# Single score banks for VectorE between ScalarE's rounds, in an attention and gated GLU kernel

## The chip, the cores and the metric

The kernel runs on one core of one Trainium2 chip. The metric is the device time of one execution in microseconds (us), lower is better. TensorE (PE), VectorE (DVE), ScalarE (ACT), GpSimd (POOL) and SyncE (SP) each work through a program of their own in order; PSUM, where TensorE's results land, is counted here in banks of 128 x 512 fp32 numbers, and there are eight.

## The reference

```python
xn = _layernorm(A_x)                       # x: 1 x 2048 x 640
# attention: 32 heads of 20
qkv = (xn @ wqkv).reshape(B, S, 3, H, Dh).transpose(2, 0, 3, 1, 4)
scores = einsum("bhqd,bhkd->bhqk", q, k) * Dh ** -0.5
o = einsum("bhqk,bhkd->bhqd", softmax(scores), v)
s = o.transpose(0, 2, 1, 3).reshape(B, S, D) @ wo
# gated GLU, F = 1728
h = sigmoid(xn @ w_gate) * (xn @ w_up)
g = silu(h @ w_down)
out = A_x + s * g
```

## The kernel before, in words

After a setup of about 30 us (layer norm, transposed activations in `xnT`, the first keys, queries and values) the main part runs over 32 passes: 4 chunks of 512 queries by 8 groups of 4 heads. A pass has 16 tiles of 128 keys for each of its 4 heads, so 64 **score banks** of 128 keys x 512 queries; 2048 in all (`NB`; the last pass is cut in two parts of 256 queries). Each bank is made by TensorE (`score`, L1155; the 4 heads lie in four groups of rows of the array, which can work side by side), turned into probabilities, and used by TensorE again (`pv`, L1289, "PV"), which adds probabilities times values in the bank `oacc`.

The exponential is made by one of two engines:

- **ScalarE**, in **rounds** (`issue`, `act_exp`): TensorE fills 3 or 2 banks in turns (`sc0`, `sc1`), and one instruction makes the exponential of all of them (L1177).
- **VectorE** (`dve_exp`): four instructions on one bank, each reading what the one before wrote. L1188 (`bits`, writes `dy`) reads the score bank and sets it free, L1193 and L1197 (`square`, `cube`, write `du`) and L1201 (`power`, writes `p`) work in SBUF.

Five PSUM banks belong to the rounds and one is `oacc`. The other two, `misc0` and `misc1`, are **shared**: a score bank for VectorE (named `spare`) takes one until L1188 has read it, and everything else that TensorE does takes one too (named `work`): keys, queries and values of later groups, the GLU's gate and up products (L644, L657), its down product (L680) and the output projection (L719, L751). A gate product's bank is freed by ScalarE's tanh (L651), most others by an eviction on VectorE (an up product by L661, which writes `hT`). The taker is `take_bank`, the freeing `give_bank`.

The order of all instructions is written by a planner in the kernel's Python, which keeps a clock for TensorE (`pe[0]`) and models VectorE and ScalarE (`Engine`: a queue of tasks, each with a length, what it depends on and a rank; the task that can start first goes first, at equal start the lower rank). A VectorE step of 512 columns counts 606 ns, with 114 ns more until a result can be used; a matmul of 512 columns counts 216 ns (`MM5`), a change between scores, PV and other work 100 ns (`INTO`); an exponential its columns / 1.2 + 52 ns. `dve.backlog` is the sum of the queued tasks' lengths, `dve.t` the time at which the running one ends.

At each step the main loop does the first of these that is possible: a round, when ScalarE's next PSUM set is free and ScalarE is about to run dry (`until` is the time at which the round is due, `room` what is left until then); a PV batch; one matmul of other work (`fill`), paced by a credit that every score bank issued adds to; a matmul on zeros that keeps TensorE's clock up (`zero_add`, L1265); else the clock moves on.

VectorE's score banks are issued in rounds alone: `issue` adds one behind ScalarE's 2 or 3, when VectorE has less than `D_BACKLOG` (2500 ns) of work and a shared bank is free. Which bank it is says `dve_bank`: the lowest of the heads' next banks that the round hasn't taken, none close to a pass's end (`NEEDED`), where one of the next pass is taken if its keys and queries are there. So that a round finds a bank, `spare_wanted` keeps other work from the last free one when the next round is near (within 800 ns, later 400) and VectorE's queue short.

Of the kernel before, what the change touches and what calls it, by code (L numbers as in the profile page):

```python
# [45 lines left out]
def kernel(  # L46
# [322 lines left out]
    MM5, MM3, MM1 = 216.0, 136.0, 70.0  # L369
# [41 lines left out]
    pe = [0.0]  # L411
# [19 lines left out]
    def pe_do(kind, took, streamed=None):  # L431
        if mode[0] != kind:
            pe[0] += INTO[kind]
            mode[0] = kind
        pe[0] += took
        if took:
            streams.append((pe[0], took if streamed is None else streamed))
# [14 lines left out]
    def take_bank(name="work"):  # L452
        ready = [i for i in range(2) if banks[i].t is not None and banks[i].t <= pe[0]]
        if not ready:
            return None
        i = min(ready, key=lambda i: banks[i].t)
        banks[i] = Cell()
        return i, psum.tile([P, QC], FP32, tag=f"misc{i}", bufs=1, name=name)
# [7 lines left out]
    def give_bank(held, cell):  # L466
        banks[held] = cell
# [603 lines left out]
    def per_bank(b):  # L1071
        todo, most = 0.0, 0.0
        for x in sorted(flight + jobs, key=lambda x: x.due):
            todo += max(0.0, x.left)
            most = max(most, todo / max(1.0, x.due - b))
        return most
# [2 lines left out]

    KEEP_SPARE, KEEP_LATE, SPARE_END, next_round = 800.0, 400.0, 20 * PER_PASS, [0.0]  # L1080
    BUFS, D_BACKLOG = {3: 4, 2: 4, 1: 3}, 2500.0
    NEEDED, NEEDED_LAST = 6, 12
    PV_TIME = 2 * MM5 + 30.0
    sets = [Cell(0.0), Cell(0.0)]
    buffers = {n: [Cell(0.0)] * BUFS[n] for n in BUFS}
# [23 lines left out]
    def lacks():  # L1109
        return list({(w[1], w[2]): w for b in coming(GH) for w in needs(b)}.values())  # L1110

    def issued(b):
        j = b % GH
        done_ahead[j].add(b // GH)
        while ahead_of[j] in done_ahead[j]:
            done_ahead[j].remove(ahead_of[j])
            ahead_of[j] += 1

    def dve_bank(banks):
        b = min((x for x in coming(GH) if x not in banks), default=None)  # L1120
        if b is None:
            return None
        ends = PER_PASS * (b // PER_PASS + 1) if b < LAST else min(e for e in ENDS if e > b)
        if ends - b > (NEEDED if ends < NB else NEEDED_LAST):
            return b
        if ends == NB:
            return None
        b = ends + b % GH
        while b // GH in done_ahead[b % GH]:
            b += GH  # L1130
        cells = [w[0].get(w[1]) for w in needs(b)]
        if any(c is None or c.t is None or c.t > pe[0] for c in cells):
            return None
        return b
# [15 lines left out]
    def score(ps, b):  # L1150
        p, r = divmod(b, PER_PASS)
        qc, g = steps[p]
        j, rows = r % GH, slice(32 * (r % GH), 32 * (r % GH) + 1 + Dh)
        for kt, q0, c0, n in pieces(b):
            nc.tensor.matmul(ps[:, c0:c0 + n], lhsT=kT_all[rows, g, kt * P:(kt + 1) * P],  # L1155
                             rhs=qTs[qc, g][rows, q0:q0 + n], start=True, stop=True, tile_position=(32 * j, 0))
# [25 lines left out]
    def dve_exp(ps, b, begun):  # L1182
        buf = Probs([b], "p1")
        t = {}

        def bits():
            t["y"] = pp.tile([P, 512], FP32, tag="dy", bufs=2, name="dy")
            nc.vector.tensor_scalar(out=t["y"], in0=ps, scalar1=LEAST, scalar2=None, op0=ALU.max)  # L1188
            t["f"] = t["y"].bitcast(U16).rearrange("p (q two) -> p q two", two=2)[:, :, 0]

        def square():
            t["u"] = pp.tile([P, 512], FP32, tag="du", bufs=2, name="du")
            nc.vector.scalar_tensor_tensor(out=t["u"], in0=t["f"], scalar=CUBE_2, in1=t["f"],  # L1193
                                           op0=ALU.add, op1=ALU.mult)

        def cube():
            nc.vector.scalar_tensor_tensor(out=t["u"], in0=t["u"], scalar=CUBE_1, in1=t["f"],  # L1197
                                           op0=ALU.add, op1=ALU.mult)

        def power():  # L1200
            nc.vector.scalar_tensor_tensor(out=buf.tile()[:, 0, :].bitcast(U16), in0=t["u"], scalar=CUBE_SCALE,  # L1201
                                           in1=t["y"], op0=ALU.mult, op1=ALU.add)

        first = dve.add(606.0, [Cell(begun + MM5 + PE_OUT - 100.0), *d_made[-2:-1]], bits, 0, 114.0)
        c = dve.add(606.0, [first, *d_made[-2:-1]], square, 3, 114.0)
        c = dve.add(606.0, [c], cube, 3, 114.0)
        buf.made = dve.add(606.0, [c, buf.before], power, 3, 114.0)
        d_made.append(buf.made)
        return first

    def issue():
# [23 lines left out]
        at_bank[0] += n  # L1235
        return n

    def pv_batch():

        p = pv_pass[0]  # L1240
        if p >= len(steps) - 1 + len(PARTS):
            return None
        if sum(pv_count[0]) == 0 and not (oacc_free[0].t is not None and oacc_free[0].t <= pe[0]):
            return None
        batch = []
        for j in range(GH):
            mine = []
            for x in ready_p[j]:
                b, buf, i = x
                if unit(b) > p or len(mine) == 2:  # L1250
                    break
                c, v = buf.made, v_cells.get((b % PER_PASS // GH, steps[min(p, len(steps) - 1)][1]))
                if c.t is not None and c.t + SEM <= pe[0] and v is not None and v.t is not None and v.t <= pe[0]:
                    mine.append(x)
            if len(mine) < 2:
                return None
            batch.append(mine)
        return batch
# [61 lines left out]
    while pv_pass[0] < len(steps) - 1 + len(PARTS):  # L1320
        advance(pe[0])
        pads()
        load_wo()
        load_bulk()
        ci, b0 = chunk[0], at_bank[0]
        p = min(b0, NB - 1) // PER_PASS
        until, stuck, can = 1e18, False, False
        if b0 < NB:
            wanted = lacks()
            late = [w[2] for w in wanted if w[0].get(w[1]) is None]  # L1330
            if late:
                must_fill(max(min(late) - 1, 0))
                continue
            cells = [w[0][w[1]] for w in wanted] + [sets[ci % 2]]
            stuck = any(c.t is None for task in act.queue for c in task[3])
            guess = pe[0] + (2000.0 if stuck else 400.0)
            free = max(c.t if c.t is not None else guess for c in cells)
            dry = max(act.t, pe[0]) + sum(t[2] for t in act.queue) - MM5 - PE_OUT + 2000.0 * stuck
            into = 0.0 if mode[0] == "score" else INTO["score"]
            until = max(free, dry - AHEAD) - into  # L1340
            can = all(c.t is not None for c in cells) and free <= pe[0] + into + 1.0
            if can and (until <= pe[0] + (0.0 if mode[0] == "score" else 40.0) or idle):
                idle = False
                n = issue()
                credit = min(credit + n * per_bank(b0), 3000.0)
                continue
        room = until - pe[0]
        next_round[0] = until
        held = sum(len(q) for q in ready_p)
        batch = pv_batch()  # L1350
        cost = PV_TIME + (INTO["pv"] if mode[0] != "pv" else 0.0)
        if batch and (cost <= room or held >= HELD):
            pv(batch)
            idle = False
            continue
        least = (0.0 if mode[0] == "fill" else INTO["fill"]) + MM3
        hurry = (b0 >= NB or stuck or any(x.due < b0 + URGENT for x in flight + jobs[:1])
                 or held >= 12 and lacks_v())
        if (credit > 0.0 or hurry) and least <= room:
            took = fill(p, room)  # L1360
            if took:
                credit -= took
                idle = False
                continue
        if b0 < NB and can and not idle:
            idle = True
            continue
        soon = [q[k][1].made.t for q in ready_p for k in range(min(2, len(q)))]
        due = min([t for t in soon if t is not None], default=pe[0]) if b0 >= NB else 1e18
        if zero_add(min(room, due - pe[0] - MM5)):  # L1370
            idle = False
            continue
        times = [until, pe[0] + 150.0] + [t + SEM for t in soon if t is not None]
        pe[0] = min(t for t in times if t > pe[0] + 1.0)
# [79 lines left out]
```

## Time and profile before

| | |
|---|---|
| time, median of 3 runs | 894.33 us (893.8 to 894.76) |
| time of the profiled execution | 894.27 us |
| its span | 892.1 us |
| busy: PE, DVE, ACT, POOL | 804.6, 840.7, 870.6, 162.0 us |
| ScalarE's exponentials (L1177) | 717, 827.9 us busy |
| VectorE's score banks (L1188) | 257 |
| granted TensorE clock | 0.998 |

The span is the time from the first to the last instruction of the profiled execution; the 2.2 us between it and that execution's time lie around it. A group's line gives the source line, engine and operation, what it writes and reads, shapes and count, then the busy time (overlaps counted once), the mean length of one instruction in ns, the idle time of the engine just before, and what ended it. An instruction's length reaches to its end, and the next of the same engine may start a little earlier, so lengths add up to more than the busy time. A line of waits gives who waited, for whom, the total in us, how often, and the longest.

### The profile page before, as it was taken

The page shows a single profiled execution, that of the slowest core. Times are in us where ns is not written, and L with a number is a line of the kernel's source. Part 1 is how long each engine was busy: PE and PEld are TensorE (multiplying, and loading weights), DVE is VectorE, ACT ScalarE, POOL GpSimd, SP SyncE. Part 2 cuts the span into 40 slices and gives each one's busy share as a digit, 9 for nine tenths or more (in the row PEclk, how much of TensorE's full clock was granted, in tenths as well). Part 3 has the DMA queues.
Part 4 walks back from the last instruction along what each step waited for, and adds up shares of the span by engine and source line. Part 5 has one row for each costly group of instructions (what it writes and reads, how often), then busy time and mean ns, then how long its engine had stood idle before and what let it go on. Part 6 is the DMA issues. An engine that isn't in the chain of part 4 may idle for free.

```text
span 892.1 us, 16911 instructions
## 1 busy us (share of the span) xinstructions
PE 804.6 (90%) x6227; PEld 290.3 (33%) x6310; DVE 840.7 (94%) x1487; ACT 870.6 (98%) x837; POOL 162.0 (18%) x305
## 2 busy tenths in 40 slices
PE   5899899998999999999899998989999898999896
PEld 3344333332223333232233332223333332233333
DVE  7799999999999999997999999999999989999997
ACT  6999999999999999999999999999999999999995
POOL 7401111111111212111101221101112220111121
PEclk9999999999999999999999999999999999999999
DMA  8113231135451234223212243313113432200012
GB/s 317 46 35 90 64 109 35 52 98 150 109 133 42 64 89 69 65 59 72 64 23 79 70 81 79 71 26 77 34 45 85 108 54 70 67 17 21 14 32 71
DMA packets 107672, 64.40 MB, mean 72 GB/s; under 512 B 80350, under 2 KB 101906, under 8 KB 107498
## 3 DMA queue, kind: packets, MB, share of 16 engines
q1 hardware_dynamic: 97382, 47.21, 19.8%
q0 software_dynamic: 10208, 16.11, 8.2%
q8 instruction: 49, 0.80, 0.4%
q14 instruction: 33, 0.27, 0.1%
HBM read 50.45 MB, written 16.13 MB: 75 GB/s over the span
## 4 chain that ended last, share of the span: by engine, by line
ACT 64%; issue 18%; PE 10%; DVE 7%; DMA 0%; SPq 0%; DVEq 0%; ACTq 0%
ACT p L1177 59%; PE sc L1155 3%; ACT tnh L651 3%; PE oacc L1289 2%; DVE dy L1188 2%; PE work L644 1%; DVE du L1193 1%; PE work L124 1%; PE work L680 1%; ACT td L691 1%; DVE stats L227 1%; DVE p L1201 1%; DVE du L1197 1%; PE work L150 1%; DMA x_sb<-in_A_x_dram 0%
## 5 line engine op out<-in xcount | busy, mean ns | idle before, releaser
L1177 ACT ACTIVATE p<-sc 128x1536 bf16<-128x1536 f32 x717 | 827.9, 1358 | 2.0 <-PE oacc L1289 1.4
L1155 PE MATMUL sc<-qT,kT_all 21*128 21x512 bf16 (+1 forms) x1848 | 280.0, 375 | 57.4 <-ACT p L1177 49.3
L1188 DVE TENSOR_SCALAR dy<-spare 128x512 f32<-128x512 f32 x257 | 175.6, 683 | 22.9 <-PE spare L1155 20.2
L1155 PEld LDWEIGHTS <-kT_all 21*128 21x128 bf16 x2112 | 91.0, 91 | 286.6 <-issue 274.6
L1197 DVE SCALAR_TENSOR_TENSOR du<-du,dy 128x512 f32<-128x512 f32 x257 | 174.4, 682 | 1.7
L1201 DVE SCALAR_TENSOR_TENSOR p<-du,dy 128x512 uint16<-128x512 f32 x257 | 174.2, 680 | 1.4
L1193 DVE SCALAR_TENSOR_TENSOR du<-dy 128x512 f32<-128x512 uint16 x257 | 174.4, 682 | 0.8
L1289 PE MATMUL oacc<-p,v_all 128*21 128x512 bf16 (+1 forms) x2112 | 157.3, 376 | 0.6 <-DVE v_all L157 0.3
L1155 PE MATMUL spare<-qT,kT_all 21*128 21x512 bf16 (+1 forms) x264 | 98.6, 378 | 0.0
L773 POOL DMA_DIRECT2D den_dram<-oev x31 | 18.0, 579 | 391.5 <-DVE oev L772 391.5
L680 PE MATMUL work<-wd,hT 128*128 128x320 bf16 x448 | 85.5, 302 | 0.1
L644 PE MATMUL work<-xnT,wg 128*128 128x512 bf16 (+1 forms) x261 | 77.6, 383 | 1.9 <-issue 0.8
L657 PE MATMUL work<-xnT,wu 128*128 128x512 bf16 (+1 forms) x268 | 73.1, 381 | 1.2 <-DVE dy L1188 0.3
L789 POOL DMA_DIRECT2D rl<-rec_dram x124 | 62.0, 512 | 57.7 <-DMA rec_dram<-den 48.0
L1265 PE MATMUL oacc<-xnT,zero 128*128 128x512 bf16 x165 | 56.0, 384 | 3.4 <-issue 2.5
L1289 PEld LDWEIGHTS <-v_all 128*21 128x21 bf16 x2112 | 31.1, 90 | 62.0 <-issue 60.1
L680 PEld LDWEIGHTS <-hT 128*128 128x128 bf16 x448 | 35.0, 97 | 48.6 <-issue 39.1
L651 ACT ACTIVATE tnh<-work 128x512 bf16<-128x512 f32 (+1 forms) x56 | 41.2, 735 | 0.0
L661 DVE SCALAR_TENSOR_TENSOR hT<-tnh,work 128x512 bf16<-128x512 bf16 (+1 forms) x56 | 37.9, 678 | 2.2 <-ACT tnh L651 2.2
L783 POOL DMA_DIRECT2D rec_dram<-den x31 | 17.0, 547 | 120.0 <-DVE den L782 115.3
L719 PE MATMUL work<-wo_pad,oT 128*128 128x320 bf16 x192 | 35.6, 302 | 0.5 <-issue 0.5
L644 PEld LDWEIGHTS <-wg 128*128 128x128 bf16 (+1 forms) x280 | 21.7, 98 | 42.8 <-issue 31.1
(123 smaller groups left out, 553.6 us busy)
## 6 DMA issues: line engine op xcount, KB each, us to landing
wg<-in_B_w_gate_dram SPq DMA_DIRECT2D x52, 160.0 KB
wu<-in_B_w_up_dram SPq DMA_DIRECT2D x52, 160.0 KB
rl<-rec_dram POOLq DMA_DIRECT2D x124, 64.0 KB, 2.5
qT<-q_dram SPq DMA_DIRECT2D x31, 128.0 KB
gq_dram<-d POOLq DMA_DIRECT2D x12, 320.0 KB, 2.5
gqr<-gq_dram SPq DMA_DIRECT2D x12, 320.0 KB
kT_all<-k_dram SPq DMA_DIRECT2D x28, 128.0 KB
wd<-in_B_w_down_dram SPq DMA_DIRECT2D x13, 160.0 KB
```

The lines of the kernel that those rows point to most:

```text
L644: nc.tensor.matmul(psg[0:fsz, :], lhsT=wg[:, kd, 0:fsz], rhs=xnT[:, kd, cols], start=(kd == 0), stop=(kd == KD - 1))
L651: nc.scalar.activation(out=made["t"][0:fsz, :], in_=psg[0:fsz, :], func=ACT.Tanh, scale=0.5)
L657: nc.tensor.matmul(psu[0:fsz, :], lhsT=wu[:, kd, 0:fsz], rhs=xnT[:, kd, cols], start=(kd == 0), stop=(kd == KD - 1))
L680: nc.tensor.matmul(psd[:, 0:HALF], lhsT=hT[0:fsz, kf, t4 * P:(t4 + 1) * P], rhs=glu[1][0:fsz, kf, e0_:e1_], start=(kf == 0), stop=(kf == N ...
L789: nc.gpsimd.dma_start(out=t["rl"][32 * j:32 * j + 32, :], in_=rec_dram[n, j:j + 1, :].to_broadcast([32, QC]))
L1155: nc.tensor.matmul(ps[:, c0:c0 + n], lhsT=kT_all[rows, g, kt * P:(kt + 1) * P], rhs=qTs[qc, g][rows, q0:q0 + n], start=True, stop=True, ti ...
L1177: nc.scalar.activation(out=buf.tile(), in_=ps, func=ACT.Exp, bias=EXP_BIAS, scale=exp_scale)
L1188: nc.vector.tensor_scalar(out=t["y"], in0=ps, scalar1=LEAST, scalar2=None, op0=ALU.max)
L1193: nc.vector.scalar_tensor_tensor(out=t["u"], in0=t["f"], scalar=CUBE_2, in1=t["f"], op0=ALU.add, op1=ALU.mult)
L1197: nc.vector.scalar_tensor_tensor(out=t["u"], in0=t["u"], scalar=CUBE_1, in1=t["f"], op0=ALU.add, op1=ALU.mult)
L1201: nc.vector.scalar_tensor_tensor(out=buf.tile()[:, 0, :].bitcast(U16), in0=t["u"], scalar=CUBE_SCALE, in1=t["y"], op0=ALU.mult, op1=ALU.add)
L1289: nc.tensor.matmul(oacc[32 * j:32 * j + 1 + Dh, q0:q0 + width], lhsT=v_all[:, kt, GH * g + j, 0:1 + Dh], rhs=buf.ap[:, i, c0:c0 + width], ...
```

## The change

A new helper, `alone`, issues one score bank for VectorE by itself, outside a round. It does so when less than 700 ns (`ALONE`) of work is queued and running on VectorE by the plan, a shared bank is free, the keys and queries of the next banks are there, the second last bank given to VectorE has its place in VectorE's order, and the matmul with the change into scores fits before the next round is due. The main loop tries it right after the rounds, ahead of PV and other work. The issued bank adds to the credit as a round's banks do. Rounds, `D_BACKLOG` and `spare_wanted` stay as they are.

```diff
-    NEEDED, NEEDED_LAST = 6, 12
+    NEEDED, NEEDED_LAST, ALONE = 6, 12, 700.0
...
+    def alone(room):
+        if (chunk[0] < 2 or (0.0 if mode[0] == "score" else INTO["score"]) + MM5 > room
+                or dve.backlog + max(0.0, dve.t - pe[0]) >= ALONE or any(c.t is None for c in d_made[-2:-1])):
+            return False
+        if any(w[0].get(w[1]) is None or w[0][w[1]].t is None or w[0][w[1]].t > pe[0] for w in lacks()):
+            return False
+        b = dve_bank([])
+        held = take_bank("spare") if b is not None else None
+        if held is None:
+            return False
+        pe_do("score", 0.0)
+        begun = pe[0]
+        score(held[1], b)
+        issued(b)
+        give_bank(held[0], dve_exp(held[1], b, begun))
+        pe_do("score", MM5)
+        at_bank[0] += 1
+        return True
...
         room = until - pe[0]
         next_round[0] = until
+        if b0 < NB and not stuck and alone(room):
+            idle = False
+            credit = min(credit + per_bank(b0), 3000.0)
+            continue
         held = sum(len(q) for q in ready_p)
         batch = pv_batch()
```

## The prediction

> **What bounds the kernel now.** I read three things in order: busy time of each engine in stretches of 25 us, the groups of instructions on the engine that has no room, and the waits of the other two. The stretches first (us, then busy us and instructions of PE, PEld, DVE, ACT, POOL; granted clock; DMA share; GB/s):
>
> ```profile
> 400.00:425.00 25.00, 23.20 (x165) 7.32 (x170) 20.31 (x35) 25.00 (x25) 3.68 (x7) 1.00 0.30 71
> 450.00:475.00 25.00, 24.01 (x185) 8.58 (x185) 23.94 (x42) 25.00 (x25) 4.22 (x8) 1.00 0.14 37
> 700.00:725.00 25.00, 22.61 (x188) 8.84 (x191) 21.44 (x38) 25.00 (x24) 6.13 (x10) 1.00 0.43 77
> sum 875.00, PE 795.44 PEld 285.61 DVE 829.46 ACT 864.24 POOL 161.04; mean PE 22.73 PEld 8.16 DVE 23.70 ACT 24.69 POOL 4.60
> ```
>
> ScalarE shows 25.00 of 25 almost everywhere from 75 us on, and VectorE doesn't. So the span is a start of about 31 us, ScalarE's exponentials without a gap, and an end of about 10 us; it shortens only if ScalarE is given fewer banks. VectorE is the one that can take them, and it has room left: of the 850 us after the first stretch (829.46 less the 19.70 of the first, 809.8) it is idle for 40.2.
>
> The groups, with shapes kept apart (count, busy us, mean ns, idle before and who ended it):
>
> ```profile
> L1177 ACT ACTIVATE p<-sc 128x1536 bf16<-128x1536 f32 x358 | 562.8, 1572 | 0.4 <-PE spare L1155 0.4
> L1177 ACT ACTIVATE p<-sc 128x1024 bf16<-128x1024 f32 x358 | 409.8, 1145 | 1.6 <-PE oacc L1289 1.4
> L1188 DVE TENSOR_SCALAR dy<-spare 128x512 f32<-128x512 f32 x257 | 175.6, 683 | 22.9 <-PE spare L1155 20.2
> ```
>
> ScalarE's exponentials waited 2.0 us in all. VectorE made 257 banks; the kernel has 32 passes of 64, so 2048, and ScalarE made the other 1791. The waits say what VectorE lacks, and what TensorE has to spare (between 30 and 870 us; total, times, longest):
>
> ```profile
> DVE dy L1188 <- PE spare L1155: 20.2, 33, 2.0
> PE sc L1155 <- ACT p L1177: 48.2, 133, 1.0
> ```
>
> Half of VectorE's idle time is 33 waits for a score bank: TensorE hadn't issued one yet.
>
> **Price of a bank on each side.** ScalarE: the page gives 827.9 us for all exponentials without their overlap; over 1791 banks that is 0.462 us each (512 columns more cost 1572 - 1145 = 0.427, the rest is the share of an instruction's fixed part). VectorE: four instructions. The timeline shows how close they stand:
>
> ```profile
> 401.22 0.68 DVE L1193 SCALAR_TENSOR_TENSOR du<-dy 128x512 f32<-128x512 uint16 x1
> 401.82 0.67 DVE L585 TENSOR_SCALAR row<-work 32x512 bf16<-32x512 f32 x1
> ...
> 407.78 0.69 DVE L1188 TENSOR_SCALAR dy<-spare 128x512 f32<-128x512 f32 x1 [1.34 <-PE spare L1155]
> 408.51 0.69 DVE L1193 SCALAR_TENSOR_TENSOR du<-dy 128x512 f32<-128x512 uint16 x1
> 409.24 0.69 DVE L1197 SCALAR_TENSOR_TENSOR du<-du,dy 128x512 f32<-128x512 f32 x1
> 409.96 0.69 DVE L1201 SCALAR_TENSOR_TENSOR p<-du,dy 128x512 uint16<-128x512 f32 x1
> ```
>
> Behind an independent instruction the next starts after 0.60 us, behind one whose result it reads after 0.73. A bank costs 4 x 0.60 = 2.4 us woven with others, 3 x 0.73 + 0.60 = 2.8 alone; I take 2.6. The plan in the code counts 606 ns a step and 114 more behind a dependence, so it knows VectorE's pace, and won't overload it by a wrong price.
>
> **How much of the wait comes back.** The stretch around a long wait (start, length):
>
> ```profile
> 766.27 0.85 ACT L651 ACTIVATE tnh<-work 128x512 bf16<-128x512 f32 x1
> ...
> 767.17 1.02 PE L644 MATMUL work<-xnT,wg 128*128 128x512 bf16 x4
> 767.26 0.68 DVE L661 SCALAR_TENSOR_TENSOR hT<-tnh,work 128x512 bf16<-128x512 bf16 x1
> 768.13 0.39 PE L1155 MATMUL sc<-qT,kT_all 21*128 21x512 bf16 x2
> 768.45 0.61 PE L1289 MATMUL oacc<-p,v_all 128*21 128x512 bf16 x8
> ...
> 769.43 0.40 PE L1155 MATMUL sc<-qT,kT_all 21*128 21x512 bf16 x3
> 769.45 0.38 PE L1155 MATMUL spare<-qT,kT_all 21*128 21x512 bf16 x1
> 769.90 0.69 DVE L1188 TENSOR_SCALAR dy<-spare 128x512 f32<-128x512 f32 x1 [1.96 <-PE spare L1155]
> ```
>
> Both shared banks held the gate and the up product. The tanh freed one and L644 took it; hT (L661) freed the other at 767.94. The round at 768.13 went without a spare bank, and VectorE's next came with the round at 769.43. The change lets a bank follow the round at about 768.45: 1.0 of the 1.96 us comes back. What lies ahead of 767.94 does not, since no bank was free. Where the bank is free earlier, nearly all comes back. I put it at 0.65 of 20.2, 13 us, and 2 us more from gaps below a wait, since the bank is asked for when under 0.7 us of work is left: 15 us, or 15 / 2.6 = 6 banks. Ends: none, and all 40.2 us at 2.4, 17 banks.
>
> So ScalarE loses 6 x 0.462 = 2.8 us (0 to 7.7). Nothing else is late next in its place: ScalarE stays full, and the end after its last exponential is the same work.
>
> **What the change adds.** A bank of its own for TensorE. In a round a further bank is nearly free: two banks at 768.13 hold TensorE for 0.32 us until PV starts at 768.45. A bank issued by itself pays such a visit whole, 0.32 us, and up to 0.1 to re-enter the work it split; directly behind a round less. With 33 waits I expect 30 to 70 such visits (many stand in for a bank of the next round, so they are more than the 6 gained): 10 to 30 us of TensorE. Cover: the 48.2 us in which it waits for ScalarE, and the clock-keeping matmuls on zeros (L1265, 165 recorded, 56.0 us). So I cost it at nothing; without that cover it would be those 10 to 30 us. The test in the code also asks that the visit end before the next round is due.
> [...]
>
> The bank's matmul waits for the shared bank's last reader; behind it in TensorE's queue stand PV, the GLU work and the next round. Such waits stand at 0.9 and 0.3 us in all before L124 and L657, none over 0.3 each: 0 to 0.3 a visit, and I take 0, as the change asks for a bank that the plan has free already. On VectorE the new bank's first step goes ahead of evictions (rank 0 against 1): an eviction, and the shared bank behind it, comes up to 0.6 us later; that falls on GLU work, with the zero matmuls as cover. The bank taken is the next in order, so its probabilities come some 3 us after their neighbours' issue and hold PV back; ScalarE has waited for PV 1.4 us in two places, so 0 to 2 us, and I take 0.3, inside the rounding of the sum. A gain is excluded for these three, as each only delays. No DMA is added, and none is moved past a queue by more than the visit.
>
> **Sum.** The profiled execution took 894.27 us, its span 892.1 and 2.2 around it; the median of the runs is 894.33, the same for this purpose. 894.3 - 2.8 = 891.5, a span of 889.3.
>
> **Rivals.**
> (1) No change that counts: the single bank only comes ahead of the bank that the next round would have given. A round comes each 1.23 us (717 rounds in some 880), and the plan refuses a round's bank while VectorE has 2.5 us queued, so the early bank is refunded later. For it: VectorE is 94% busy, and both shared banks may be held when it runs dry. Against: in the stretch above 1 us of real idle time goes. It gives 0 to 3 banks, up to 1.4 us: 893 to 894.3.
> (2) Slower: the visits make ScalarE's rounds late. TensorE waited for ScalarE before only 133 of 717 rounds; before the others it came when it came, and a visit of 0.32 us ahead of such a round is 0.32 us in which ScalarE is dry. It decides from 2.8 / 0.32 = 9 such visits on. Half of 50 visits: 8.0 us lost, 2.8 gained, 899.5; all of 70 without gain, 916. Against it: the test for room, TensorE's 48.2 us, and that the plan counts 1332 ns for a 1536-column exponential, where the pair of 1536 and 1024 columns takes 827.9 / 358 = 2.31 us against 2.24 in the plan, so on the chip TensorE gains on ScalarE all the time. [...]
> (3) VectorE filled to the brim, the end of my own case: 17 banks, 886.6.
>
> **Chances.** A measurement of this kernel can tell about 0.2%, 1.8 us, from no change. My forecast with (3) as its tail: 0.60, of which 0.04 gains less than 1.8 us. (1): 0.20. (2) and smaller losses of its kind (late GLU work, early K and Q work near 30 us pushed back by a taken bank): 0.20, of which 0.02 within 0.2%. So faster 0.56, same 0.26, slower 0.18. The range reaches from 888.0 (14 banks) to 898.0, which takes in the milder half of (2); my case alone is 888 to 893.
>
> **What would show it.** Right: L1188 at 260 to 268 instead of 257, L1177 at about 715; idle before L1188 down from 22.9 to about 10; ScalarE still 25.00 in each stretch; spare matmuls without sc matmuls beside them. Wrong: L1188 unchanged with shorter waits (1); idle before L1177 up from 2.0 by several us, released by PE (2); fewer L1188, if single banks keep the shared banks from the rounds.

## The result and the profile after

The changed kernel is slower: 896.22 us median of 22 runs against 894.34 of 22 runs before, ratio 1.0038 (95% interval 1.002 to 1.0056). Its runs lie in three groups: six at 893.6 to 894.4 us, nine at 895.8 to 897.4, seven at 902.9 to 904.8. The kernel before stays within 893.8 to 896.6. The profiled execution is one of the last group: 903.05 us, span 900.9.

The groups of the page first, in the columns of the page before:

```profile
L1177 ACT ACTIVATE p<-sc 128x1536 bf16<-128x1536 f32 x714 | 825.4, 1351 | 11.9 <-PE sc L1155 8.0
L1188 DVE TENSOR_SCALAR dy<-spare 128x512 f32<-128x512 f32 x263 | 180.0, 685 | 19.2 <-PE spare L1155 16.4
```

VectorE has 263 banks instead of 257 and ScalarE three rounds less, as forecast. But ScalarE's idle time before its exponentials went from 2.0 to 11.9 us. The busy times in stretches of 25 us say where (columns as in the prediction: PE, PEld, which is the loading of weights into TensorE's array, DVE, ACT, POOL, granted clock, DMA share, GB/s):

```profile
200.00:225.00 25.00, 22.49 (x102) 4.13 (x103) 16.61 (x31) 16.36 (x15) 1.99 (x4) 0.56 0.43 110
225.00:250.00 25.00, 22.78 (x160) 7.18 (x160) 21.87 (x37) 24.23 (x24) 3.68 (x7) 0.96 0.43 113
```

The granted clock fell to half in one place before the end, and ScalarE lost 8.6 us in that stretch and 0.8 in the next; from 75 us on it shows 24.80 or more of 25 in every other stretch up to 875. What stands ahead of it, in the waits between 30 and 880 us:

```profile
PE work L644 <- DMA wg<-in_B_w_gate_dram: 1.7, 1, 1.7
```

The wait of L644 for its weights is new. TensorE's timeline around it, and SyncE's for the load:

```profile
198.44 1.29 PE L124 MATMUL work<-xnT,wqd 128*120 128x512 bf16 x5
199.66 0.39 PE L1155 MATMUL sc<-qT,kT_all 21*128 21x512 bf16 x2
201.73 0.60 PE L644 MATMUL work<-xnT,wg 128*128 128x512 bf16 x2 [1.68 <-DMA wg<-in_B_w_gate_dram]
```

```profile
198.46 0.46 SPq L620 DMA_DIRECT2D wg<-in_B_w_gate_dram  x1
```

L644 at 201.73 is the first gate product of the whole kernel. Its weights were requested at 198.46 and TensorE came to it at 200.05; it stood still for 1.68 us. In the kernel before the same load went out at 191.31, and TensorE had more to do ahead of L644 (three rounds, PV and matmuls on zeros, of which some lines):

```profile
191.31 0.45 SPq L620 DMA_DIRECT2D wg<-in_B_w_gate_dram  x1
...
192.83 0.39 PE L1265 MATMUL oacc<-xnT,zero 128*128 128x512 bf16 x1
...
193.55 0.61 PE L1289 MATMUL oacc<-p,v_all 128*21 128x512 bf16 x8
...
194.78 0.59 PE L644 MATMUL work<-xnT,wg 128*128 128x512 bf16 x2 [0.26 <-DVE dy L1188]
```

That is 3.47 us from issue to use there and 3.27 here. In five profiles in which TensorE waits for weights loaded this way, the first matmul starts 3.2 to 3.3 us after the issue (in a sixth, further down, 4.6), so the kernel before had them just in time by luck. The plan knows nothing of this load: `load_glu` issues it without a landing time, and any job may follow at once. The change issues 14 single banks in all (counted in the plan), two of them within the first 25 us of the main part. The GLU work starts 7 us later, at a place where, besides the five matmuls of L124 that stand there in both, one round alone comes between the load and its use; that the two early banks do this is tested below.

### The profile page after: what moved, and what is told of

It is laid out like the page before. It is cut to its first block, busy times and chain, and to the rows that moved or that the text cites. A ratio compares the mean times of both kernels' runs of the same rounds, so it can differ in the third digit from the quotient of the medians.

```text
span 900.9 us, 16880 instructions
## 1 busy us (share of the span) xinstructions
PE 810.9 (90%) x6202; PEld 288.8 (32%) x6282; DVE 855.0 (95%) x1511; ACT 869.4 (97%) x834; POOL 162.2 (18%) x305
## 4 chain that ended last, share of the span: by engine, by line
ACT 57%; issue 16%; PE 14%; DVE 11%; DMA 1%; SPq 0%; ACTq 0%; DVEq 0%
ACT p L1177 53%; PE sc L1155 4%; PE oacc L1308 2%; ACT tnh L651 2%; DVE dy L1188 2%; DVE du L1193 2%; PE work L644 2%; DVE du L1197 2%; DVE p L1201 1%; PE work L124 1%; DVE stats L227 1%; PE work L657 1%; PE oacc L1284 1%; DVE hT L661 1%; ACT td L691 1%
## 5 line engine op out<-in xcount | busy, mean ns | idle before, releaser
L1177 ACT ACTIVATE p<-sc 128x1536 bf16<-128x1536 f32 x714 | 825.4, 1351 | 11.9 <-PE sc L1155 8.0
L1188 DVE TENSOR_SCALAR dy<-spare 128x512 f32<-128x512 f32 x263 | 180.0, 685 | 19.2 <-PE spare L1155 16.4
L1197 DVE SCALAR_TENSOR_TENSOR du<-du,dy 128x512 f32<-128x512 f32 x263 | 179.1, 683 | 1.9
L1201 DVE SCALAR_TENSOR_TENSOR p<-du,dy 128x512 uint16<-128x512 f32 x263 | 179.0, 682 | 1.5
L1193 DVE SCALAR_TENSOR_TENSOR du<-dy 128x512 f32<-128x512 uint16 x263 | 179.0, 683 | 0.6
L1308 PE MATMUL oacc<-p,v_all 128*21 128x512 bf16 (+1 forms) x2112 | 159.2, 380 | 0.7 <-DVE v_all L157 0.7
L1155 PE MATMUL spare<-qT,kT_all 21*128 21x512 bf16 (+1 forms) x270 | 101.7, 381 | 0.2
L644 PE MATMUL work<-xnT,wg 128*128 128x512 bf16 (+1 forms) x260 | 77.7, 389 | 2.9 <-DMA wg<-in_B_w_gate_dram 1.7
L1284 PE MATMUL oacc<-xnT,zero 128*128 128x512 bf16 x144 | 49.3, 391 | 2.0 <-issue 1.9
L657 PEld LDWEIGHTS <-wu 128*128 128x128 bf16 (+1 forms) x280 | 24.1, 98 | 38.1 <-issue 21.1
```

What stands on the lines that cost most here:

```text
L644: nc.tensor.matmul(psg[0:fsz, :], lhsT=wg[:, kd, 0:fsz], rhs=xnT[:, kd, cols], start=(kd == 0), stop=(kd == KD - 1))
L657: nc.tensor.matmul(psu[0:fsz, :], lhsT=wu[:, kd, 0:fsz], rhs=xnT[:, kd, cols], start=(kd == 0), stop=(kd == KD - 1))
L1177: nc.scalar.activation(out=buf.tile(), in_=ps, func=ACT.Exp, bias=EXP_BIAS, scale=exp_scale)
L1308: nc.tensor.matmul(oacc[32 * j:32 * j + 1 + Dh, q0:q0 + width], lhsT=v_all[:, kt, GH * g + j, 0:1 + Dh], rhs=buf.ap[:, i, c0:c0 + width], ...
```

## Experiments

Theory A: the late weights cost the change its gain, by the wait itself and by the clock that may halve behind it. Theory B: single banks and fewer matmuls on zeros thin TensorE's stream, and the clock falls where it is thin. Four rivals are tested on the way: C, single banks make ScalarE's rounds late; D, the spread of the times comes from elsewhere, such as DMA or the order of waits, and the clock only follows; E, more matmuls on zeros get in the way of scores; F, an early load helps by itself.

**The changed kernel again.**

> The changed kernel, unchanged, for a second profile and more times. All theories: times in three groups as before, near 893.8, 896.2 and 903. Theory A (the first gate product reaches TensorE before its weights; TensorE stands still for 1.7 us, and in some executions the granted clock halves behind it): the profile shows TensorE waiting 1.5 to 1.8 us for wg near 201 us and ScalarE idle 1.5 us behind it; where the clock falls at all, it falls right there. Theory B (single banks and fewer matmuls on zeros thin the stream of matmuls, and the clock falls wherever it's thin): the clock falls at other places too.

Twelve runs: seven at 893.5 to 894.3, three at 895.9 to 897.8, two at 904.3 and 904.9. The profiled execution is of the first group (893.79, span 891.7), so it shows the change with its clock whole. Its groups, and ScalarE's and TensorE's waits:

```profile
L1177 ACT ACTIVATE p<-sc 128x1536 bf16<-128x1536 f32 x714 | 824.6, 1353 | 4.0 <-PE oacc L1308 2.2 <-PE sc L1155 1.5
L1188 DVE TENSOR_SCALAR dy<-spare 128x512 f32<-128x512 f32 x263 | 179.9, 684 | 15.6 <-PE spare L1155 13.0
```

```profile
ACT p L1177 <- PE oacc L1308: 2.2, 2, 1.6
ACT p L1177 <- PE sc L1155: 1.5, 1, 1.5
...
PE work L644 <- DMA wg<-in_B_w_gate_dram: 1.7, 1, 1.7
```

ScalarE's exponentials fell by 3.3 us (827.9 to 824.6), and its idle time before them rose by 2.0, of which 1.5 is one round behind the wait for wg. So the wait is there in an execution with a whole clock too, and takes back about half of the gain. Whether the clock then falls differs between executions of the same order. Here are the same stretches of both executions, the disturbed one first:

```profile
199.60:203.00 3.40, 1.72 (x16) 0.42 (x15) 2.39 (x4) 1.88 (x3) 0.52 (x2) 1.00 0.95 214
203.00:226.90 23.90, 23.07 (x101) 4.19 (x99) 14.63 (x27) 16.64 (x15) 1.47 (x3) 0.50 0.34 93
```

```profile
199.60:203.00 3.40, 1.74 (x16) 0.40 (x14) 2.21 (x4) 1.90 (x3) 0.71 (x2) 1.00 0.97 218
```

TensorE was busy for 1.72 us of 3.40 in the one and 1.74 in the other; in the one the clock was halved for the next 23.9 us, in the other not until the end of the kernel.

The clock's own steps in the traces say what differs. In the disturbed execution the clock is whole for 184.32 us up to the fall at 202.97, half for 23.89, and whole for 672.43 up to the fall at the end (899.29); in the profile of the kernel before it is whole for 870.40 us up to the fall at the end (888.41). These are 54, 7, 197 and 255 times 3.413 us. Laid off in windows of that length from the steps of its own clock, the wait of the disturbed execution lies in one window (199.56 to 202.97, TensorE busy for 1.73 us), and that of the undisturbed one is shared by two:

```profile
197.23:200.64 3.41, 2.22 (x19) 0.86 (x11) 3.41 (x8) 3.41 (x4) 0.55 (x1) 1.00 0.40 92
200.64:204.05 3.41, 2.53 (x19) 0.63 (x19) 1.50 (x3) 1.91 (x3) 1.76 (x4) 1.00 0.95 226
```

So two nearly equal stretches, with unlike places in these windows, had unlike outcomes. That the place decides is my reading of these two executions; no run varies it alone. In the 23.90 us at half clock TensorE's record, in which the ends of matmuls are modelled, is busy for 23.07.

**The weights early, in the change and in the kernel before.**

```diff
+    gw = ctx.enter_context(tc.tile_pool(name="gw", bufs=2, side="right", reuse_waits="tile"))
     early = ExitStack()
...
-        wg = glu[0].tile([P, KD, P], BF16, tag="wg", bufs=WB, name="wg")
+        wg = gw.tile([P, KD, P], BF16, tag="wg", bufs=WB, name="wg")      # wu alike
...
-        for kf in range(WB - 1):
-            load_glu(0, kf)
...
     at(12000.0, last_bound)
+    at(100000.0, lambda: load_glu(0, 0))
```

> The changed kernel with the first gate and up weights loaded some 60 us earlier, into buffers that no earlier tile uses; the order of every instruction on TensorE, VectorE and ScalarE stays the same. Theory A: no wait for wg, clock as in the kernel before in every execution, one group of times near 892.3 (893.8 less 1.5), faster than before by 0.2%. Theory B: the stream of matmuls is as thin as it was, so the three groups stay, 892.3 to 903. Theory C (single banks make ScalarE's rounds late): 893.6 or more, with idle time before L1177 spread over the run.

> The kernel before with the first gate and up weights loaded some 60 us earlier, all else in its order. Theory A: the kernel before didn't wait for these weights, so 894.2 to 894.5 as before. Rival F (the early load helps in general, by moving bytes out of a busy stretch): faster by 1 us or more, as it was with the change.

The change with early weights: 892.54 us median of 12, ratio to the kernel before 0.9986 (0.9973 to 0.9999). The wait for wg is gone; seven runs lie at 891.9 to 892.6, five at 893.0 to 899.1. The kernel before with early weights: 894.32, ratio 1.0002 (0.9993 to 1.001), so early weights are worth nothing by themselves (F falls), and 1.6 to 1.7 us in the change (893.5 to 894.3 undisturbed against 891.9 to 892.6): the price of the wait. The group above 902 us is gone as well: none of the 12 runs lies there, where 9 of 34 of the change do. Theory A's one group near 892.3 didn't come, though; the five longer runs have clocks of 0.989 to 0.997. C falls in this profile: outside PV, ScalarE waited for score banks once in the whole run:

```profile
ACT p L1176 <- PE oacc L1307: 2.2, 2, 1.6
ACT p L1176 <- PE sc L1154: 0.8, 1, 0.8
```

(Lines stand one or so lower or higher in edited kernels.) That wait, at 462 us, lies in a spell of 3.4 us at half clock far from any late load, so theory A isn't all:

```profile
456.40:459.80 3.40, 2.36 (x22) 0.66 (x19) 3.37 (x6) 3.40 (x4) 0.57 (x1) 1.00 0.48 123
459.80:463.30 3.50, 3.50 (x19) 0.76 (x16) 3.31 (x6) 2.72 (x3) 0.57 (x1) 0.52 0.05 9
```

**The weights late, in the kernel before.**

```diff
+        load = lambda: nc.sync.dma_start(out=wg[:, :, 0:fsz], ...)
+        load() if c + kf else late_load.append(load)
...
+        if late_load:
+            late_load.pop()()
         wg, wu = glu_w.pop((c, kf))
```

> The kernel before with the first gate weights loaded fourth instead of first (behind the up weights and both weights of the next step), everything else in the same order. Theory A: TensorE waits 1 to 2 us for wg near 195 us, ScalarE is idle 1 to 1.7 us behind it, and the time has groups as the change has: about 895.5 undisturbed, 898 and 905 where the clock falls. Theory B: no single banks, so the clock stays, and all times lie near 895.5.

899.78 us median of 5 runs (899.65 to 901.39), ratio 1.0066 (1.0054 to 1.0078). The order of every other instruction is that of the kernel before. The wait is 1.9 us, and all five have a lower clock (0.991 to 0.993). The profiled execution:

```profile
194.60:198.00 3.40, 1.53 (x11) 0.42 (x14) 0.96 (x5) 1.78 (x2) 0.57 (x1) 1.00 0.82 200
198.00:201.40 3.40, 3.40 (x17) 0.55 (x9) 2.86 (x7) 2.48 (x2) 0.00 (x0) 0.50 0.02 5
201.40:204.80 3.40, 3.40 (x11) 0.55 (x10) 1.77 (x4) 2.22 (x2) 0.85 (x2) 0.50 0.06 14
204.80:208.20 3.40, 3.40 (x19) 0.80 (x15) 2.77 (x4) 3.00 (x4) 1.69 (x4) 0.50 0.46 125
```

One load that comes late by 1.9 us leaves TensorE 1.53 us of 3.40 and costs 5.5 us of span, without a single bank by itself anywhere: theory A shown from the other side. I had expected an undisturbed group at 895.5; there was none. By my estimate, if the windows of 3.41 us lay anywhere with equal chance, which no run shows, a wait of 1.9 us would lie whole in one of them in fewer than half of the runs (1.5 of 3.41), so five of five isn't explained by its place alone; that stays open.

**Only the early banks, only the later ones.** The condition in the main loop gets `not glu and` in the first kernel, `glu and` in the second.

> Single banks only until the GLU work starts: two, both within the first 25 us of the main part, which shift the start of the GLU work by 7 us and put the first gate product right behind its load; afterwards none (256 banks on VectorE, 717 rounds, 207 matmuls on zeros). Theory A: TensorE waits 1.5 to 1.8 us for wg near 201 us as in the change, without the change's gain: 895.5 to 896.5 undisturbed, in groups up to 906. Rival D (the two early banks have nothing to do with it; the wait comes from the later ones): 894.4, no wait for wg.

> The change from the start of the GLU work on only, so that the order until then, and the distance of the first gate product from its weights, is that of the kernel before. It issues 26 single banks (the change issues 14), and VectorE makes 262 banks in all, ScalarE 715 rounds against 717. Theory A: no wait for wg, clock as before, 257 - 262 = 5 banks less on ScalarE at 0.46 us: 892.0. Theory B: more single banks than the change, so the clock falls more often: over 896. Theory C: 26 visits instead of 14, so ScalarE's idle time grows: 894 or more.

Two early banks alone: 898.14 us median of 6 (896.65 to 899.92), ratio 1.0045 (1.0034 to 1.0056), with TensorE's wait for wg of 1.6 us. So the harm comes from the two banks that bring no gain (256 banks on VectorE, 717 rounds), and the theory that the later ones bring the wait (D, as it is put for this run) falls. The harm is larger than the wait: in the profiled execution, 3.7 us longer in span, ScalarE is idle for 2.3 us more between its first and last exponential, is busy for 0.9 more there (its other work beside no exponential, tanh for the most part, takes 22.5 us instead of 20.0, the exponentials 826.3 instead of 827.9), and the end is 0.7 us longer.

The later banks alone, 26 of them by the plan, reach the forecast in their best and profiled execution: 891.46, span 889.5, where the forecast had 891.5 and 889.3.

```profile
L1177 ACT ACTIVATE p<-sc 128x1536 bf16<-128x1536 f32 x715 | 823.8, 1341 | 2.2 <-PE oacc L1308 1.4 <-PE spare L1155 0.4 <-PE sc L1155 0.2
L1188 DVE TENSOR_SCALAR dy<-spare 128x512 f32<-128x512 f32 x262 | 178.7, 684 | 12.9 <-PE spare L1155 7.7 <-PE sc L1155 1.9
```

But the twelve runs spread from 891.46 to 899.35 (median 894.23, ratio 1.0004, 0.9988 to 1.002), with clocks of 0.989 to 0.999 that follow the times. Theory B's "over 896" is wrong for the median, theory A's 892.0 for most runs, and C's 894 for the fastest five (891.5 to 893.9), with no round of the profiled one later than 0.4 us for its scores.

**The stream of matmuls on zeros.** The plan holds TensorE's stream at `ENOUGH` = 2500 ns in 3400 by adding matmuls on zeros: 220 in the kernel before, 192 in the change. Only this number is changed, 2900 in three kernels and 2200 in one.

> The kernel before, without any single bank, with the floor of the stream lowered to 2200 ns in 3400 (118 matmuls on zeros instead of 220; 256 banks on VectorE, 717 rounds). Theory B: the clock falls in some executions though there are no single banks and no late weights: 894.4 undisturbed, several between 895.5 and 900. Rival D: 894.3 to 894.8 in all.

> The kernel before with the floor at 2900 ns (382 matmuls on zeros; 256 banks on VectorE, 717 rounds). Theory B: no execution above 894.9, where some of the kernel before lie at 895.3 to 896.6; median 894.3 to 894.8, as ScalarE has the same work. Rival E: slower than before by 1 us or more.

> The changed kernel with early first weights, and with the plan's floor for TensorE's stream raised from 2500 to 2900 ns in 3400 (367 matmuls on zeros instead of 192; 261 banks on VectorE, 715 rounds). Theory B (what is left of the spread is the clock, which falls where the plan leaves the stream thin): all executions within 0.7 us, clock 0.998 or more, 257 - 261 = 4 banks less on ScalarE: 892.4. Rival D (the spread comes from elsewhere, from DMA or the order of waits, and the clock only follows the idle time): the spread of 892 to 899 stays. Rival E (more matmuls on zeros come in the way of scores): over 894.

> Single banks from the start of the GLU work on only, with the floor of the stream at 2900 ns (371 matmuls on zeros instead of 190; 261 banks on VectorE, 715 rounds). Theory B: the spread of 891.5 to 899.4 goes, all within 0.7 us of 892.2, clock 0.998. Rival D: spread as it was. Rival E: over 894.

With fewer zeros the kernel before takes 901.2 us median (899.5 to 911.8; ratio 1.0097, 1.0059 to 1.0134), clocks 0.978 to 0.997. Its profile (911.74, clock 0.978) has no wait for wg and one spell of 34.1 us at half clock, from 143.2 us on. So the clock does fall without single banks and without late weights. But the fastest run, at 0.997, is still 5 us behind the kernel before, so the new order costs time besides the clock; in the profile the end behind the last exponential takes 13.9 us instead of 10.7.

With more zeros I was wrong three times. Before with 2900: 903.04 (900.0 to 906.1; ratio 1.0099, 1.0075 to 1.0123), 900 even at a clock of 0.999. The change with early weights and 2900: 897.43 (ratio 1.0045, 1.0031 to 1.0059). From the GLU work on and 2900: 901.8 (ratio 1.0073, 1.0054 to 1.0092). Rival E holds, and cleanest in the change with early weights, where TensorE doesn't wait for wg: four of its six runs have clocks of 0.998 and 0.999 and take 896.8 to 897.8, 5 us more than with the floor at 2500 (of which two banks fewer on VectorE are 0.9). TensorE's slack fits with it. In the kernel before with a floor of 2900:

```profile
PE sc L1155 <- ACT p L1177: 16.3, 57, 0.8
...
PE work L644 <- DMA wg<-in_B_w_gate_dram: 1.6, 1, 1.6
```

TensorE waits 16.3 us for ScalarE instead of 49.1 (30 to 880 us), and ScalarE's idle time between its first and last exponential is 6.7 us instead of 2.7. And the new order put the first gate product behind its load once more, as it did in the third kernel (1.6 us there too).

Theory B isn't borne out by the higher floor: the spread stays, as D had it (896.8 to 901.5 and 897.2 to 903.2). The profile of the change with early weights and 2900 shows one reason why a floor in the plan doesn't help: its one fall, at 684 us (clock 0.997 over the span), stands behind a wait of TensorE of 1.8 us for VectorE, which has itself waited 2.1 us for a DMA (`den`) that the plan takes to have landed.

**A small step up instead, 2600.**

> The changed kernel with early first weights and the floor of the stream at 2600 ns instead of 2500 (263 banks on VectorE, 714 rounds, 208 matmuls on zeros instead of 192). Theory B: fewer executions with a fallen clock than with early weights alone, where 5 of 12 lay above 892.9; median 892.0 to 892.5. Rival E (matmuls on zeros are in the way): 893 or more at full clock.

> Single banks from the start of the GLU work on, floor of the stream 2600 ns (261 banks on VectorE, 715 rounds, 220 matmuls on zeros, as many as before the change, instead of 190). Theory B: the spread of 891.5 to 899.4 shrinks to 891.5 to 894; median under 893. Rival D: as wide as it was.

The change with early weights: 892.5 us median of 11, ratio 0.999 (0.998 to 1.0001); eight at 891.8 to 892.8, three at 895.4 to 896.2: no clear difference to 2500. From the GLU work on: 899.82 (ratio 1.0063, 1.0046 to 1.0079), against all expectation. In its profile, where the GLU work starts at another place again, TensorE waits 2.0 us before the first L644, ScalarE is idle for 2.0 us behind it, and 6.8 us at half clock follow (clock 0.995 over the span):

```profile
PE work L644 <- DVE du L1197: 2.0, 1, 2.0
PEld L644 <- DMA wg<-in_B_w_gate_dram: 2.3, 1, 2.3
```

The first line puts the matmul's wait down to VectorE, which happened to finish `du` just then (L644 doesn't read it). The second, of the load of the same product's weights into the array (PEld), names what was missing: `wg`, issued at 201.71 and there at 206.30, 4.6 us later. It is the late weights once more.

**Does the clock fall behind single banks?** In the first kernel below nothing is changed; in the second, the change with early weights, a single bank adds nothing to the plan's count of the stream (`pe_do("score", MM5, 0.0)`).

> Single banks from the start of the GLU work on, unchanged, for a second profile: 891.5 to 899.4 again, two of three executions disturbed. If single banks thin the stream, the clock falls within some 3.4 us behind a single bank; if it is any place where TensorE waits, it falls behind a wait of 0.7 us or more for ScalarE or a shared bank, with no single bank near.

> The changed kernel with early first weights, where a single bank no longer counts toward the plan's floor of the stream (263 banks on VectorE, 714 rounds, 208 matmuls on zeros instead of 192). If single banks are what is counted too high: nearly all executions between 891.9 and 892.6, where 5 of 12 were above 892.9 without this. If not: as many above as before.

The first ran at 893.6 to 896.8 in ten runs (ratio 1.0016, 1.0007 to 1.0025); its one profile is of an execution that took 1342 us at a clock of 1.000, and can't answer this. The second: 893.62 median (892.6 to 896.5, ratio 1.0, 0.999 to 1.0011), no better than with the bank counted, and its profile shows another wait of TensorE, 2.0 us before a gate product, for VectorE.

The profiles of the other runs say more. Six kernels with single banks show a fall in the middle, at 203, 460, 208, 199, 684 and 405 us. With the plan's single banks found again among VectorE's banks in the traces, the nearest one ahead of any of these falls is some 15 us away (445 us, ahead of 460); the others are 98 us away and more, or haven't come yet. The two profiles with the most single banks, 26 and 21, have no fall in the middle. So in no profile does the clock fall right behind a single bank. What does stand in the 3.41 us ahead is, in five of the eight falls of all profiles, one wait of TensorE of 1.6 to 2.0 us: four times for `wg`, once for VectorE behind a DMA. The other three have no single wait over 0.95 us. That fewer matmuls on zeros (192 instead of 220 in the plan) make the change more prone to them isn't shown.

## Why the prediction was wrong

**What bounds the kernel, the prices, and the gain** were right. A bank costs ScalarE 0.46 us; 6 banks moved, as forecast. VectorE's idle time from 25 to 875 us fell from 40.2 to 25.3 us in the execution with the clock whole, the 15 us of the forecast. The exponentials fell by 3.3 us against 2.8, but ScalarE's other work beside no exponential grew by 0.8, so its gain is 2.5. The time of 891.46 with the later banks alone is the forecast's to 0.1 us partly by luck: 5 banks moved there instead of 6, ScalarE worked 2.2 us less, and 0.4 came from idle time. With the change and early weights the undisturbed runs are at 891.9 to 892.6.

**The number of single banks** was wrong: 14 instead of 30 to 70. The plan's VectorE is short of work and a shared bank free at once far less often than the trace's 33 waits suggest. That 14 visits brought as many banks as were expected of 30 to 70 is luck too: VectorE's idle time before L1188 fell from 22.9 to 15.6 us, not to the forecast 10, and the other half of the 15 us came back at other places.

**"Nothing else is late next in its place", and of DMA "none is moved past a queue by more than the visit"**, are the step that failed. I priced the visit and not the plan: two early visits moved the start of the GLU work by 7 us and took away the work that had stood between the first weight load and its use. The first gate product started 3.47 us behind its load before, and in five profiles the load took 3.2 to 3.3. A margin so small is to be read from the timeline of before, and I didn't look at loads at all. It cost 1.5 us of ScalarE's time even with the clock whole. The sum of that execution: exponentials 3.3 less, idle time between the first and the last of them 1.7 more (4.3 against 2.7), other ScalarE work beside no exponential 0.8 more, the end behind the last one 0.4 longer (11.1 against 10.7); 0.4 us of span are left (892.1 to 891.7).

**The clock** was no term of the sum, and no rival had this loss: (2) has ScalarE's rounds late, but from the visits; with the clock whole the only round late for its scores was the one behind the load. The chances name "late GLU work" among smaller losses, without a price. TensorE's 1.7 us of standing still cost 9 us more in one profiled execution (903.05) than in the other (893.79), and what the two traces show to differ is where it lay in the windows of 3.41 us: in one with TensorE busy for 1.73 us, or in two with 2.22 and 2.53. Of the 22 runs, the 16 outside the first group have clocks of 0.983 to 0.996 against 0.999; where the clock fell in those without a profile isn't known, and the falls that stay with early weights show that it isn't always here. The median lies inside 888 to 898, seven of the 22 runs don't, and the sign is the other one.

**The cover of the visits**, costed at nothing because the matmuls on zeros would give way, is in doubt: with 118 of those matmuls instead of 220 the kernel before ran at clocks of 0.978 to 0.997 instead of 0.998 and 0.999. Whether the 28 that gave way in the change cost anything no run shows; one execution with 192 has its clock whole (0.999).

Two ends are off in the last digit, and nothing rests on them: 17 banks at 0.462 are 7.9 us and give 886.4, and 70 visits of 0.32 us give 916.7.

## What to carry to other kernels

In a kernel whose order is written by a planner, a change at one place reorders all that follows: read from the profile which loads and waits are just in time now, and give the planner their landing times before anything else. A wait of under 2 us on the matrix engine can have a spell at a lower clock behind it and cost several times its length, and not in every execution (here, with the same wait of 1.7 us, 903.05 us in one and 893.79 in another): look at the spread of the runs and the granted clock, not at a median of three. Where a matmul's wait is put down to an engine whose result it doesn't read, look at the wait of its weight load as well. Filler work wasn't slack here, and more of it wasn't free either: the kernel before took 901.2 us with 118 matmuls on zeros and 903.04 with 382, against 894.2 with 220.

## What the runs showed of the hardware

- The profile of the change has the clock whole for 184.32 us, half for 23.89 and whole for 672.43, that of the kernel before whole for 870.40: 54, 7, 197 and 255 times 3.413 us. The other spells at half clock named above lasted 3.4 us (the change with early weights), 6.8 (from the GLU work on, 2600), 10.2 (the kernel before with late weights) and 34.1 (the kernel before with fewer zeros).
- In the 3.40 us ahead of a fall TensorE's record was busy for 1.53 us (the kernel before with late weights), 1.72 (the change) and 2.36 (the change with early weights). No fall came behind the windows with 2.22 and 2.53 in the second profile of the change.
- The spells behind these three lasted 10.2, 23.9 and 3.4 us, so their length doesn't follow from the busy time ahead. TensorE's record was nearly full in the first two (10.20 of 10.20 us, 23.07 of 23.90), and the clock was at half all the same.
- A load of 160 KB on SyncE's queue, with three more behind it, let its first matmul start 3.2 to 3.3 us after issue in five profiles, and 4.6 us in one.
